# Attention sinks as bf16 products of three parts, split on GpSimd and VectorE, and ranks as sums of signs on ScalarE

## The chip, the core and the metric

The kernel runs on one core of a Trainium2 chip. A core has a matrix engine (TensorE; PE in the profile, with PEld for the loads of its weights), a vector engine (VectorE, DVE), an activation engine (ScalarE, ACT), a general-purpose engine (GpSimd, POOL) and a queue engine (SyncE, SP). Each runs its own instructions in the order in which they were issued; semaphores tie them together. DMA transfers are issued from the queues of SP, ACT and POOL. The metric is the time of one execution on the device, in microseconds; lower is better.

## The reference

Attention with a sliding window and four sinks for 4 batches of 8 heads, 768 positions of 64 values; then a mixture of depths: in each batch the 128 rows with the highest gate score go through a two-layer network, and the others are left as they are.

```python
scores = scale * np.matmul(q, k.transpose(0, 1, 3, 2))
keep = is_sink | in_window            # first 4 positions, or the last 128
scores = np.where(keep, scores, -1000000000.0)
a = np.exp(scores - np.max(scores, axis=-1, keepdims=True))
a = a / (np.sum(a, axis=-1, keepdims=True) + 1e-09)
x = np.matmul(a, v)                   # heads side by side: B, S, 512
...
scores = np.einsum('bsd,d->bs', x, w_gate)
top_idx = np.argpartition(-scores[b], capacity)[:capacity]
h = np.maximum(x[b, top_idx] @ w1, 0.0)
g = 1.0 / (1.0 + np.exp(-scores[b, top_idx]))
out[b, top_idx] = x[b, top_idx] + g[:, None] * (h @ w2)
```

## The kernel before

The work is written out in a fixed order of 30 entries, the list `steps`. Batch 0 takes entries 0 to 11, with two of the four head groups at a time (g = 0, then g = 1, for each of six blocks of 128 queries); batches 1 to 3 take six entries each, all heads at once (12 to 17, 18 to 23, 24 to 29). The loop over `steps` (L728 to L763) does the same in each entry: a store of the rows finished before, the scores of the entry two ahead (`step_scores`, with one or two exponentials of 1024 columns on ACT, L296), then `values` (the products of probabilities and values, fp32, L307, and of the sinks, L318, into PSUM banks X and X+1, the same in every entry), then `norm` (a reciprocal, L347, and two multiplications, L350, on DVE), then the gate score of the finished rows (L354). Other work is hung on an entry by four lists: `before` (ahead of the entry), `middle` (ahead of `values`), `at` (behind `norm`) and `late` (at the end).

**Loads and transposes.** K and Q of a pair of heads come by `load_pair` (L150, on SP's queue) into `raw`, are cast to bf16 on POOL (`cast_pair`, L185), turned by PE (`transposes`, L52) into PSUM banks Y and Y+1, and copied from there to KT and QT by DVE or ACT (L222, L224). The loads are held back by a list `plan`: its k-th group is issued once 188 + 256 k units of PE work have been issued (`Counted`; an fp32 product counts four, a bf16 product or a transpose two), which is called mark k.

**Sinks.** `sink_keys` (L231, POOL) copies the first four columns of KT into `ksk`, so that one product with Q gives the scores of the sinks of several heads, 64 rows for each half of the query columns. `sink_scores` does these products and one exponential into `psk` (fp32). The values of the sinks lie in `vsk` (fp32, rows 0 to 15, loaded by four DMAs of POOL's queue, L521; the copy for rows 64 to 79 is made by POOL, L725). In `values`, `sinks()` multiplies 64 rows of both; in all entries that have sinks, but for one, these are the first products of the entry.

**Ranks.** A row is chosen if fewer than 128 scores of its batch are higher. For batches 0 and 1 the gate scores go to DRAM and come back as a row on all partitions (`bounce_out`, `bounce_in`); `rank_c` (L364, DVE) counts, for each of six columns, how many of 768 are greater. For batches 2 and 3 the row is made by PE (`spread`) and compared block by block (`compare`, `overtake`). `select` and `chosen` make the indices; `gather`, `ffn_*`, `ffn_out` and `scatter` do the network and write the chosen rows over those in DRAM. `gate` and `gate_end` make the sigmoid from the chosen scores, `token_cols` puts a score into two bf16 columns.

**The end.** Behind the loop stands the selection of batch 3, the rest of batch 2's network, `ffn_out(1)` and `scatter(1)`, then those of batches 2 and 3. All scatters write `out` and are done one after the other.

Of the kernel before, what the change touches and what calls it, by code (L numbers as in the profile page):

```python
# [15 lines left out]
B = 4  # L16
H = 8
S = 768
# [37 lines left out]
def kernel(  # L56
# [29 lines left out]
    vsk = one([128, B, 2, HP, SK], FP32, "vsk")  # L86
    ksk = [one([128, HP, 64], BF16, f"ksk{i}") for i in range(2)]
# [5 lines left out]
    pskb = [one([128, 2, 5 * 64], FP32, f"psk{i}") for i in range(2)]  # L93
    x0 = one([128, NB, DM], FP32, "x0")
    scolb = [one([128, NB], FP32, f"scol{i}") for i in range(B)]
    xb = x0[:, 0:NB // 2, :].bitcast(BF16).rearrange("p a (t n) -> p (a t) n", t=2)
    E2 = x0[:, NB - 1, :].bitcast(BF16)[:, 0:NB * 128].rearrange("p (c n) -> p c n", n=128)
    sbc = one([128, S], FP32, "sbc")
    sbl = one([128, S], FP32, "sbl")
# [3 lines left out]
    rankl = [one([128, NB], FP32, "rankl"), x0[:, NB - 2, 40:40 + NB]]  # L103
# [9 lines left out]
    hT = one([128, 8, 128], BF16, "hT")  # L113
    w1_sb = one([128, 4, FF], BF16, "w1_sb")
# [5 lines left out]
    zb = one([128, 512], BF16, "zb")  # L120
# [7 lines left out]
    tk_i = one([128, B + 1, NB], I32, "tk_i")  # L128
    flat = out.rearrange("b s d -> (b s) d")
    srow = tc.dram_tile([B, S], FP32, name="srow")  # L130
    xrow = tc.dram_tile([S, DM], FP32, name="xrow")
    idl = x0[:, NB - 2, 0:1].bitcast(U32)

    class State:
        def __init__(self, b):
            self.b = b
            self.KT, self.QT = KTb[b % 2], QTb[b % 2]
            self.ksk = ksk[b % 2]
            self.v = vbuf[b % 2]
            self.scol = scolb[b]  # L140
            self.psk = pskb if b == 0 else [pskb[(b + 1) % 2]] * 2
# [84 lines left out]
    def sink_keys(b, hp):  # L226
        s = st[b]
        for e in range(2):
            r = slice(64 * e, 64 * e + 64)
            c0 = NSINK * (2 * (hp % 2) + e)  # L230
            pool.tensor_copy(out=s.ksk[r, hp, c0:c0 + NSINK], in_=s.KT[r, hp, 0:NSINK])  # L231

    def sink_scores(b, hps, which, bank):
        s = st[b]
        for hp in hps:
            g = hp // 2
            mine = [h for h in hps if h // 2 == g]
            for c in range(2):
                o = 64 * (g ^ c)
                q2 = s.QT[:, hp, 128:S].rearrange("p (j c n) -> p j c n", c=2, n=64)[:, :, c, :]  # L240
                pe.matmul(out=ps[o:o + 64, bank + c, 0:320], lhsT=s.ksk[:, hp, :], rhs=q2,
# [56 lines left out]
    def values(b, j, heads, bank, which):  # L298
# [13 lines left out]
        def sinks():  # L312
            for be in range(2):
                for c in range(2):
                    if j < 2 - c:
                        continue
                    r = (LO, HI)[be ^ c]
                    pe.matmul(out=ps[64 * c:64 * c + 64, bank + be, a * SK:z * SK],  # L318
                              lhsT=s.psk[which][r, c, 64 * (j - 1):64 * j], rhs=vsk[r, b, be, a:z, :],
# [40 lines left out]
    def bounce_in(b):  # L360
        pool.dma_start(out=sbc[:, :], in_=srow[b, :].partition_broadcast(128))

    def rank_c(b, c):
        dve.tensor_scalar(out=junk[:, :].bitcast(BF16)[:, 0:S], in0=sbc[:, :], scalar1=st[b].scol[:, c:c + 1],  # L364
                          scalar2=0.0, op0=ALU.is_gt, op1=ALU.add, accum_out=rank[:, c:c + 1])
# [39 lines left out]
    def token_cols(b, c0=0, c1=NB):  # L405
        t, sc = tok[b][:, c0:c1, :], st[b].scol[:, c0:c1]
# [430 lines left out]
```

## Time and profile before

| | |
|---|---|
| three runs | 147.26, 144.94, 147.16 us; median 147.16 |
| profiled execution | 144.75 us |
| its span on the engines | 142.8 us, 6432 instructions |
| PE busy | 121.2 us (85%) |
| DVE busy | 92.8 us (65%) |
| ACT busy | 77.6 us (54%) |
| POOL busy | 63.2 us (44%) |
| mean granted PE clock | 0.956 |
| DMA | 32.42 MB, 227 GB/s |

The costliest groups of instructions (line, engine, operation, output and inputs with their shapes, number | busy us, mean ns | idle time before them and what ended most of it):

```profile
L296 ACT ACTIVATE pt<-ps 128x1024 f32<-128x1024 f32 x48 | 47.2, 1025 | 14.7 <-PE ps L49 14.6
...
L49 PE MATMUL ps<-vbuf,pt 64*64 64x65 f32 (+1 forms) x1440 | 47.6, 232 | 0.9 <-issue 0.5
L185 POOL CAST kq<-raw 128x768 bf16<-128x768 f32 x28 | 24.8, 893 | 29.1 <-DMA raw<-in_k_dram 17.7
...
L350 DVE TENSOR_TENSOR x<-ps,rz 128x256 f32<-128x256 f32 (+1 forms) x60 | 19.5, 366 | 1.2
...
L49 PE MATMUL ps<-vsk,psk 64*64 64x260 f32 (+1 forms) x180 | 16.1, 366 | 0.6 <-DVE x L350 0.6
...
L364 DVE TENSOR_SCALAR_CACHE_REDUCE junk<-sbc,scol 128x768 bf16<-128x768 f32 x12 | 12.1, 1012 | 1.3 <-DMA sbc<-srow 0.9
```

All PE products carry the line of the wrapper, L49, and the transposes L52, so they are told apart by their tiles: `vsk,psk` are the products of the sinks, `vbuf,pt` those of the values, `QT,KT` the scores. An fp32 product shows as two instructions. The busy time of PE counts overlapping products once; many run side by side in quarters or halves of the array (the `64*64` in a line).

### The profile page before, as it was taken

How to read it: one execution, taken by the hardware profiler on the slowest of the kernel's cores; microseconds unless marked ns; L12 is line 12 of the kernel's file. 1: busy time of each engine (PE TensorE's matmuls, PEld its weight loads, DVE VectorE, ACT ScalarE, POOL GpSimd, SP SyncE). 2: the span in 40 equal slices, each digit the busy share in tenths (PEclk: the TensorE clock that was granted, in tenths of full speed). 3: DMA queues.
4: the chain of work that ended last, by engine and by line, in shares of the span. 5: the costliest groups of instructions: out<-in, count | busy, mean ns of one | idle time of the engine just before them, and what ended most of it. 6: DMA issues, size and time to landing. Idle time of an engine off the chain costs nothing. (4 is left out here: it accounts for less than half of the span.)

```text
span 142.8 us, 6432 instructions
## 1 busy us (share of the span) xinstructions
PE 121.2 (85%) x2763; PEld 92.6 (65%) x2763; DVE 92.8 (65%) x295; ACT 77.6 (54%) x106; POOL 63.2 (44%) x109
## 2 busy tenths in 40 slices
PE   6768989499998799999699579997999979999900
PEld 2347666478777578777577448776787758676800
DVE  6881643337847474696999623889996888784510
ACT  1577736466978877845857540675744624233100
POOL 7968520698418263141655070634150465225220
PEclk9999999969999999999999955999999999999996
DMA  3998959996999998899686997699998674341311
GB/s 101 358 221 313 276 121 258 392 349 175 318 312 339 264 326 232 211 333 309 239 236 178 287 184 228 144 193 202 260 279 189 230 276 155 145 154 25 122 73 73
DMA packets 42300, 32.42 MB, mean 227 GB/s; under 512 B 26897, under 2 KB 37137, under 8 KB 42273
## 3 DMA queue, kind: packets, MB, share of 16 engines
q1 hardware_dynamic: 38528, 26.22, 62.1%
q0 software_dynamic: 2656, 5.02, 15.5%
q10 hardware_dynamic: 1088, 0.79, 1.8%
q8 instruction: 21, 0.34, 0.9%
q14 instruction: 7, 0.05, 0.1%
HBM read 25.20 MB, written 8.92 MB: 239 GB/s over the span
## 5 line engine op out<-in xcount | busy, mean ns | idle before, releaser
L296 ACT ACTIVATE pt<-ps 128x1024 f32<-128x1024 f32 x48 | 47.2, 1025 | 14.7 <-PE ps L49 14.6
L49 PEld LDWEIGHTS ps<-vbuf,pt 64*64 64x64 f32 (+1 forms) x1440 | 40.9, 140 | 12.0 <-issue 8.8
L49 PE MATMUL ps<-vbuf,pt 64*64 64x65 f32 (+1 forms) x1440 | 47.6, 232 | 0.9 <-issue 0.5
L185 POOL CAST kq<-raw 128x768 bf16<-128x768 f32 x28 | 24.8, 893 | 29.1 <-DMA raw<-in_k_dram 17.7
L347 DVE RECIPROCAL rz<-ps 128x8 f32<-128x8 f32 (+1 forms) x30 | 5.9, 197 | 30.9 <-PE ps L49 30.7
L49 PE MATMUL ps<-QT,KT 64*64 64x192 bf16 (+2 forms) x384 | 18.5, 247 | 3.0 <-ACT sbl L370 0.9
L52 PE MATMUL ps<-ident_b,kq 128*128 128x128 bf16 x192 | 15.4, 228 | 6.0 <-POOL kq L185 3.7
L350 DVE TENSOR_TENSOR x<-ps,rz 128x256 f32<-128x256 f32 (+1 forms) x60 | 19.5, 366 | 1.2
L52 PEld LDWEIGHTS <-kq 128*128 128x128 bf16 x192 | 11.8, 102 | 9.9 <-POOL kq L185 4.4
L354 DVE CUSTOM_DVE_ANT_0 junk<-x,wgb 128x512 f32<-128x512 f32 x24 | 17.7, 736 | 0.5
L49 PE MATMUL ps<-mask,ident_b 64*64 64x256 bf16 (+2 forms) x224 | 16.6, 259 | 0.7 <-issue 0.7
L49 PE MATMUL ps<-vsk,psk 64*64 64x260 f32 (+1 forms) x180 | 16.1, 366 | 0.6 <-DVE x L350 0.6
L49 PEld LDWEIGHTS <-KT 64*64 64x64 bf16 x384 | 11.4, 108 | 6.8 <-issue 4.9
L224 ACT COPY QT<-ps 128x768 bf16<-128x768 bf16 x14 | 11.3, 809 | 4.6 <-PE ps L52 3.7
L364 DVE TENSOR_SCALAR_CACHE_REDUCE junk<-sbc,scol 128x768 bf16<-128x768 f32 x12 | 12.1, 1012 | 1.3 <-DMA sbc<-srow 0.9
L231 POOL COPY ksk<-KT 64x4 bf16<-64x4 bf16 x32 | 6.3, 197 | 13.8 <-DMA xe<-out_dram,idx 5.1
L370 ACT COPY sbl<-ps 128x128 f32<-128x128 f32 x12 | 3.1, 262 | 13.0 <-PE ps L49 12.9
L49 PEld LDWEIGHTS <-ident_b 64*64 64x64 bf16 x240 | 9.4, 111 | 0.9 <-issue 0.9
L222 DVE COPY KT<-ps 128x768 bf16<-128x768 bf16 x8 | 7.6, 953 | 1.7 <-PE ps L52 1.7
L49 PEld LDWEIGHTS ps<-vsk,psk 64*64 64x64 f32 x180 | 6.9, 135 | 2.7 <-DVE x L350 0.9
L49 PE MATMUL ps<-xeT,w_sb 128*128 128x128 bf16 x128 | 7.9, 219 | 0.0
L49 PE MATMUL ps<-w_sb,hT 128*128 128x512 bf16 (+1 forms) x40 | 7.6, 337 | 0.0
(100 smaller groups left out, 135.7 us busy)
## 6 DMA issues: line engine op xcount, KB each, us to landing
out_dram<-x SPq DMA_DIRECT2D x24, 256.0 KB, 4.5
raw<-in_k_dram SPq DMA_DIRECT2D x14, 384.0 KB, 5.4
raw<-in_q_dram SPq DMA_DIRECT2D x14, 384.0 KB, 5.2
vbuf<-in_v_dram SPq DMA_DIRECT2D x33, 128.0 KB, 5.2
w_sb<-in_moe_w_dram POOLq DMA_DIRECT2D x8, 256.0 KB, 7.1
xrow<-x SPq DMA_DIRECT2D x6, 256.0 KB, 3.3
vbuf<-in_v_dram SPq DMA_DIRECT2D x2, 384.0 KB, 5.4
sbc<-srow POOLq DMA_DIRECT2D x2, 384.0 KB, 5.8
```

The lines of the kernel that those rows point to most:

```text
L49: self.counted(self.engine.matmul(**kw), 4 if kw["lhsT"].dtype == FP32 else 2)
L52: self.counted(self.engine.transpose(**kw), 2)
L185: (eng or pool).tensor_copy(out=o, in_=i)
L222: dve.tensor_copy(out=o, in_=i)
L224: act.copy(out=o, in_=i)
L231: pool.tensor_copy(out=s.ksk[r, hp, c0:c0 + NSINK], in_=s.KT[r, hp, 0:NSINK])
L296: act.activation(out=po[:, gi, :, :, :], in_=sc[:, :, :, :], func=ACT.Exp, scale=0.125)
L347: dve.reciprocal(out=rz[:, :, 0:n, :], in_=xg[:, :, :, D:D + 1])
L350: dve.tensor_tensor(out=xo[:, e, :, :], in0=xg[:, e, :, 0:D], in1=rz[:, e, 0:n, :].to_broadcast((128, n, D)), op=ALU.mult)
L354: dve.tensor_tensor_reduce(out=junk[:, :], in0=x, in1=wgb[:, :], scale=1.0, scalar=0.0, op0=ALU.mult, op1=ALU.add, accum_out=st[b].scol[:, ...
L364: dve.tensor_scalar(out=junk[:, :].bitcast(BF16)[:, 0:S], in0=sbc[:, :], scalar1=st[b].scol[:, c:c + 1], scalar2=0.0, op0=ALU.is_gt, op1=A ...
L370: act.copy(out=sbl[:, j * 128:(j + 1) * 128], in_=ps[:, bank, 0:128])
```

## The change

Five things change together.

1. **Sinks of batches 1 to 3.** Values and probabilities of the sinks are each split into bf16 parts whose sum is the fp32 number, and the parts are laid over 128 rows (eight groups of 16), so that one bf16 product over 128 rows takes the place of an fp32 product over 64. `sink_keys` writes eight copies of the columns; `sink_parts` computes one pair of head pairs at a time and its exponential; `sink_split` makes the parts of half of the query columns with four DVE operations (`in_parts`). The values are loaded by a memset and eight DMAs on POOL ahead of entry 2 (`sink_values`), doubled to 32, 64 and 128 rows by two ACT copies (`sink_rows_double`) and split on POOL with four operations a batch, at the end of entries 6, 9 and 14 (`sink_value_parts`). Batch 0 keeps its way; its memset, loads and copy shrink to its own part.
2. **Ranks of batches 0 and 1** are ACT's sum of the sign of the difference, one activation a column, with `rank_end` on DVE; batch 1's row goes to a buffer of its own.
3. **Order.** The transposes of batch 1 move from entries 6, 7, 8, 9 to 8, 8, 9, 9, with their casts; `plan` is rewritten (K and Q earlier, V later for batch 1).
4. **Gate.** The sigmoid is taken in `token_cols` for all rows and its two bf16 parts are chosen along; `gate` is one addition and `gate_end` is gone.
5. **The end.** `ffn_out(1)` and `scatter(1)` move ahead of the last selection.

```diff
-    vsk = one([128, B, 2, HP, SK], FP32, "vsk")
-    ksk = [one([128, HP, 64], BF16, f"ksk{i}") for i in range(2)]
+    vsk0 = one([128, 2, HP, SK], FP32, "vsk0")
+    vskb = [None] + [one([128, 2, HP, SK], BF16, f"vskb{i}") for i in range(1, B)]
+    ksk = [one([128, HP, 128], BF16, f"ksk{i}") for i in range(2)]
+    parts = one([128, 4], FP32, "parts")
...
+        n = 4 if b == 0 else 8
         for e in range(2):
             r = slice(64 * e, 64 * e + 64)
             c0 = NSINK * (2 * (hp % 2) + e)
-            pool.tensor_copy(out=s.ksk[r, hp, c0:c0 + NSINK], in_=s.KT[r, hp, 0:NSINK])
+            o = s.ksk[r, hp, 0:16 * n].rearrange("p (n c) -> p n c", n=n)
+            if b == 0:
+                pool.tensor_copy(out=o[:, 0, c0:c0 + NSINK], in_=s.KT[r, hp, 0:NSINK])
+            else:
+                pool.tensor_copy(out=o[:, :, c0:c0 + NSINK],
+                                 in_=s.KT[r, hp, 0:NSINK].unsqueeze(1).to_broadcast((64, n, NSINK)))
+
+    def in_parts(x, rough, out, row, eng):
+
+        eng.tensor_scalar(out=rough, in0=x, scalar1=parts[:, row:row + 1], scalar2=0.0, op0=ALU.mult, op1=ALU.add)
+        eng.tensor_tensor(out=x, in0=x, in1=rough, op=ALU.add)
+        eng.tensor_scalar(out=rough, in0=x, scalar1=parts[:, row + 1:row + 2], scalar2=0.0, op0=ALU.mult, op1=ALU.add)
+        eng.tensor_tensor(out=out, in0=x, in1=rough, op=ALU.add)
+
+    def sink_parts(b, g, bank):
+        s = st[b]
+        for hp in (2 * g, 2 * g + 1):
+            for c in range(2):
+                q2 = s.QT[:, hp, 128:S].rearrange("p (j c n) -> p j c n", c=2, n=64)[:, :, c, :]
+                pe.matmul(out=ps[:, bank + c, 0:320], lhsT=s.ksk[:, hp, :], rhs=q2, start=hp % 2 == 0,
+                          stop=hp % 2 == 1, skip_group_check=True)
+        x = pskb[0][:, :, :]
+        act.activation(out=x, in_=ps[:, bank:bank + 2, 0:320], func=ACT.Exp, scale=0.125)
+
+    def sink_split(b, g, c):
+        in_parts(pskb[0][:, c, :], xe[2][:, 0:160].bitcast(BF16), st[b].pskh[:, g, c, :], 0, dve)
...
-                    r = (LO, HI)[be ^ c]
-                    pe.matmul(out=ps[64 * c:64 * c + 64, bank + be, a * SK:z * SK],
-                              lhsT=s.psk[which][r, c, 64 * (j - 1):64 * j], rhs=vsk[r, b, be, a:z, :],
+                    if b:
+                        lhsT, rhs = s.pskh[:, be, c, 64 * (j - 1):64 * j], vskb[b][:, be, a:z, :]
+                    else:
+                        r = (LO, HI)[be ^ c]
+                        lhsT, rhs = s.psk[which][r, c, 64 * (j - 1):64 * j], vsk0[r, be, a:z, :]
+                    pe.matmul(out=ps[64 * c:64 * c + 64, bank + be, a * SK:z * SK], lhsT=lhsT, rhs=rhs,
...
-        pool.dma_start(out=sbc[:, :], in_=srow[b, :].partition_broadcast(128))
+        pool.dma_start(out=sbcs[b][:, :], in_=srow[b, :].partition_broadcast(128))
 
     def rank_c(b, c):
-        dve.tensor_scalar(out=junk[:, :].bitcast(BF16)[:, 0:S], in0=sbc[:, :], scalar1=st[b].scol[:, c:c + 1],
-                          scalar2=0.0, op0=ALU.is_gt, op1=ALU.add, accum_out=rank[:, c:c + 1])
+
+        act.activation(out=x0[:, NB - 1, :].bitcast(BF16)[:, 0:S], in_=sbcs[b][:, :], func=ACT.Sign, scale=-1.0,
+                       bias=st[b].scol[:, c:c + 1], accum_out=rank[:, c:c + 1])
+
+    def rank_end():
+        dve.tensor_scalar(out=rank[:, :], in0=rank[:, :], scalar1=-0.5, scalar2=0.5 * (S - 1), op0=ALU.mult, op1=ALU.add)
...
-        t, sc = tok[b][:, c0:c1, :], st[b].scol[:, c0:c1]
-        dve.tensor_copy(out=t[:, :, 2], in_=sc)
-        dve.tensor_tensor(out=t[:, :, 3], in0=sc, in1=t[:, :, 2], op=ALU.subtract)
+
+        t, g = tok[b][:, c0:c1, :], gcol[:, c0:c1]
+        act.activation(out=g, in_=st[b].scol[:, c0:c1], func=ACT.Exp, scale=-1.0)
+        dve.tensor_scalar_add(out=g, in0=g, scalar1=1.0)
+        dve.reciprocal(out=g, in_=g)
+        dve.tensor_copy(out=t[:, :, 2], in_=g)
+        dve.tensor_tensor(out=t[:, :, 3], in0=g, in1=t[:, :, 2], op=ALU.subtract)
...
-        plan = [[lambda: load_pair(0, 3), lambda: load_v_first(2)],
-                [load_gate, P(1, 0), P(1, 1)],
-                [P(1, 2), P(1, 3), V(1, 0)],
-                [P(2, 0), V(1, 1)],
-                [P(2, 1), V(1, 2)],
-                [P(2, 2), V(1, 3)],
-                [P(2, 3), V(1, 4)],
-                [V(1, 5), V(1, 6), V(2, 0)],
-                [P(3, 0), V(2, 1)],
-                [P(3, 1), V(2, 2)],
-                [P(3, 2), V(2, 3)],
-                [P(3, 3), V(2, 4)],
-                [V(2, 5), V(2, 6), V(3, 0), W(0)],
-                [V(3, 1), W(1), W(2)],
-                [V(3, 2), W(3), W(4)],
-                [V(3, 3), W(5), W(6)],
-                [V(3, 4), V(3, 5), W(7)],
-                [V(3, 6)]]
+        plan = [[lambda: load_pair(0, 3), load_gate, lambda: load_v_first(2)],
+                [P(1, 0), P(1, 1)],
+                [P(1, 2), P(1, 3)],
+                [P(2, 0), P(2, 1)],
+                [V(1, 0), V(1, 1), P(2, 2)],
+                [P(2, 3), V(1, 2)],
+                [V(1, 3), V(1, 4), P(3, 0)],
+                [V(1, 5), V(1, 6), P(3, 1)],
+                [V(2, 0), V(2, 1), P(3, 2)],
+                [V(2, 2), P(3, 3)],
+                [V(2, 3), V(2, 4)],
+                [V(2, 5), V(2, 6), W(0)],
+                [V(3, 0), V(3, 1), W(1)],
+                [V(3, 2), W(2), W(3)],
+                [V(3, 3), W(4), W(5)],
+                [V(3, 4), W(6), W(7)],
+                [V(3, 5), V(3, 6)]]
...
-        for b, i, js in ((0, 12, (15, 15, 16, 17, 17, 18)), (1, 18, (20, 21, 22, 23, 24, 25))):
+        for b, i, js in ((0, 12, (15, 16, 16, 17, 17, 18)), (1, 18, (21, 22, 22, 23, 23, 24))):
...
-        for b, i0 in ((1, 6), (2, 12), (3, 18)):
-            for hp in range(HP):
-                before(i0 + hp - 1, lambda b=b, hp=hp: cast_pair(b, hp))
-                middle(i0 + hp, lambda b=b, hp=hp: transposes(b, hp, Y))
-                at(i0 + hp, lambda b=b, hp=hp: sink_keys(b, hp))
-            at(i0 + 4, lambda b=b: sink_scores(b, range(HP), 0, Y))
+        for b, at_ in ((1, (8, 8, 9, 9)), (2, (12, 13, 14, 15)), (3, (18, 19, 20, 21))):
+            for hp, i in enumerate(at_):
+                (late if b == 1 and hp == 3 else before)(i - 1, lambda b=b, hp=hp: cast_pair(b, hp))
+                (at if hp and i == at_[hp - 1] else middle)(i, lambda b=b, hp=hp: transposes(b, hp, Y))
+                at(i, lambda b=b, hp=hp: sink_keys(b, hp))
+            for g in range(2):
+                i = (9, 14, 20)[b - 1] + 2 * g
+                at(i, lambda b=b, g=g: sink_parts(b, g, Y))
+                for c in range(2):
+                    late(i + c, lambda b=b, g=g, c=c: sink_split(b, g, c))
...
+        def sink_values():
+
+            pool.memset(vsf[:, :], 0.0)
+            for r in range(2):
+                for hh in range(HP):
+                    r0 = 16 * r + NSINK * hh
+                    pool.dma_start(out=vs[r0:r0 + NSINK, :, :, hh, 0:D].rearrange("p b e d -> p (b e) d"),
+                                   in_=v4[hh, 0:NSINK, 1:B].rearrange("s b e d -> s (b e) d"))
+
+        def sink_rows_double(n):
+            act.copy(out=vsf[n:2 * n, :], in_=vsf[0:n, :])
...
+        def sink_value_parts(b):
+            n = 2 * HP * SK
+            in_parts(vsf[:, (b - 1) * n:b * n], w2_sb[:, :, :].rearrange("p c f -> p (c f)")[:, 0:n],
+                     vskb[b][:, :, :, :].rearrange("p e h w -> p (e h w)"), 2, pool)
+        before(2, sink_values)
+        for n in (32, 64):
+            late(5, lambda n=n: sink_rows_double(n))
+        late(5, sink_rows)
+        for b, i in ((1, 6), (2, 9), (3, 14)):
+            late(i, lambda b=b: sink_value_parts(b))
...
         compare_own(b, NB - 1)
+        ffn_out(1, Y + 1)
+        scatter(1)
         overtake((NB - 1,), 3)
...
-        ffn_out(1, Y + 1)
-        scatter(1)
         ffn_2(2, 0, 0)
         ffn_2(2, 1, 0)
         ffn_out(2, 0)
         scatter(2)
-        gate_end(b)
         ffn_1(b, 0, Y)
```

Not shown: the setting up of the row masks and of the per-row factors `parts` (`sink_rows`, eleven small POOL operations and two of DVE, at the end of entry 5), buffers that are laid over others, and the two lines that take `gate_end` away.

## The prediction

> **What bounds the kernel now.** I number the 30 entries of `steps` 0 to 29 and mark step i's end by its reciprocal in `norm` (L347), R(i). I read the slices first:
>
> ```profile
> PE   6768989499998799999699579997999979999900
> DVE  6881643337847474696999623889996888784510
> ...
> PEclk9999999969999999999999955999999999999996
> ```
>
> PE is nearly always busy, except around slices 7 and 22, and just behind each hole PEclk falls to half. Windows laid over those places:
>
> ```profile
> 24.80:28.20 3.40, 1.34 (x19) 1.07 (x21) 1.42 (x3) 1.31 (x2) 2.05 (x5) 0.95 1.07 392
> 28.20:31.60 3.40, 3.40 (x46) 2.74 (x43) 1.37 (x5) 1.98 (x3) 3.02 (x5) 0.55 1.05 365
> ...
> 79.20:82.60 3.40, 1.34 (x38) 0.96 (x38) 2.45 (x10) 2.51 (x5) 0.46 (x1) 0.98 1.01 297
> 82.60:86.00 3.40, 2.97 (x35) 2.01 (x37) 0.56 (x4) 1.18 (x2) 2.12 (x4) 0.50 0.93 171
> 86.00:89.40 3.40, 3.40 (x78) 2.94 (x79) 1.33 (x6) 0.27 (x1) 0.00 (x0) 0.51 0.77 230
> ```
>
> (PE, PEld, DVE, ACT, POOL busy; then clock.) About 2 us of idle PE in 3.4 us costs a further 3.4 or 6.8 us at half clock: 1.7 and 3.4 us lost. The waits and the timeline name the cause, input loads that reach POOL's casts late:
>
> ```profile
> POOL kq L185 <- DMA raw<-in_k_dram: 17.7, 8, 4.5
> ...
> PE ps L52 <- POOL kq L185: 3.7, 3, 1.6
> ```
> ```profile
> 20.60 0.40 POOL L231 COPY ksk<-KT 64x4 bf16<-64x4 bf16 x2 [2.21 <-DVE KT L222]
> 22.14 0.46 PE L49 MATMUL ps<-QT,ksk 128*64 128x320 bf16 x4
> 25.48 0.82 POOL L185 CAST kq<-raw 128x768 bf16<-128x768 f32 x1 [4.47 <-DMA raw<-in_k_dram]
> 26.36 0.51 PE L52 MATMUL ps<-ident_b,kq 128*128 128x128 bf16 x6 [1.59 <-POOL kq L185]
> ```
>
> Between the holes PE and DVE alternate, because `values` always writes the same two PSUM banks: it can't start before the previous `norm` is done. Two steps (same columns):
>
> ```profile
> 91.90:95.78 3.88, 3.88 (x107) 2.93 (x108) 3.51 (x11) 2.80 (x4) 2.11 (x5) 1.00 1.07 172
> 95.78:99.49 3.71, 3.00 (x66) 2.26 (x66) 3.57 (x11) 2.18 (x3) 1.43 (x2) 1.00 1.09 178
> ```
>
> DVE fills 3.5 us of 3.7 to 3.9; 1.0 of it is one rank. The end is a row of scatters on POOL, each held until the one before has landed:
>
> ```profile
> 131.13 1.02 POOL L486 DMA_INDIRECT out_dram<-y,idx  x1 [0.30 <-issue]
> ...
> 134.74 1.00 POOL L486 DMA_INDIRECT out_dram<-y,idx  x1 [2.59 <-DVE hT L468]
> ...
> 138.26 0.98 POOL L486 DMA_INDIRECT out_dram<-y,idx  x1 [2.51 <-DMA out_dram<-y,idx]
> ```
>
> **What the Trainium skill says.** "TensorE: Matmul & The Clock Gate", Part 1: after an idle window of about 3.4 us the array runs at half clock. The trace agrees (0.55 and 0.50, in units of 3.4 us). "SBUF — State Buffer", "Who interferes with whom": a VectorE instruction with two SBUF inputs and a GpSimd instruction that reads SBUF exclude one another. The trace fits: the 6-column subtraction of L408 takes 0.77 us beside a cast, where the 5-column one takes 0.17.
>
> **The change, part by part.** The sum is made against the profiled execution: span 142.8, 144.75 us in all, which is 2.4 below the median 147.16 and under all three runs.
>
> *Removed or relieved.*
> - The waits of steps 6 and 7: no transposes stand there any more. Gaps of 1.59 and 0.50, and 1.7 of half clock: **-3.8**.
> - R(20) to R(21) takes 9.32 us (78.68 to 88.00), beside 4.3 for the step before. The last loads of batch 3 are released two marks earlier, so that the cast should find its data: about -4.7.
> - Sinks of batches 1 to 3: 8 instructions of a step take 0.60 us (115.89 to 116.49). In bf16 there are 4, over 128 rows. The fp32 value products have the same two column halves: 64 in 1.64 us, 26 ns each for 65 columns in two passes, so 260 columns in one pass cost twice that, and 4 take 0.2. PE saves 0.4 in each of 13.5 steps. Eight score products per batch go from 64 to 128 columns wide and lose pairing: 0.73 to about 1.1.
> - 12 ranks of 1.03 us leave DVE for ACT. In exchange DVE gets 12 splits of four 128x320 operations. Cast-like: 344 ns at 384, so 0.30; two-input: 419 at 256, so 0.48; a split is 1.55. DVE's work is 4.5, 4.2, 4.3 and 4.4 in steps 20 to 23, where a step took 3.7 to 3.9 apart from the hole; there the PE saving is worth nothing.
> - Step by step, the larger of PE's and DVE's work from R(14) to R(29) is 4.0+3.7+3.5+4.3+3.3+4.4+4.6+4.6+4.6+4.4+4.0+4.9+4.9+3.7+5.0 = 63.9, against 69.0 now (54.57 to 123.60). PE's work is the present step less 0.3 to 0.4, plus 0.5 with `sink_parts`; DVE's is norm 0.98, gate score 0.77, split 1.55, KT copy 0.95, and the comparisons of the trace, where the step has them. **-5.1**, the hole included; R(13) to R(14) **-0.3**.
> - The tail: `scatter(1)` goes out about 4 us earlier, so `scatter(2)` follows its y (132.93) at once, and the last scatter waits for its own y (136.3) instead of 138.26: -1.7. The moved y (0.75, half hidden by a PE wait) and two more gate operations add 0.7 ahead of `chosen`. **-1.0**.
> - Costed at nothing: the smaller start-up memset (DVE waits for POOL's bands until 3.90 in any case); the gate load in front of `load_v_first(2)` (0.54 of SP's queue; those values are needed from step 6, some 5 us after they land; with that cover gone, 0.5); V(1,0) and V(1,1) at mark 4, behind step 9's products: 5.2 to land, about 7 until values(12) asks for them, else the difference is a stall; the weights, a mark earlier on POOL.
>
> *Added.*
> - **A.** POOL gets a memset of 1560 and eight DMAs behind the cast that ends at 18.03, ahead of the `ksk` copies of pairs 1 and 3. Memset: 0.10 for one column, 0.20 for 128, so 1.35. DMAs: L521's median of 0.617, so 4.9. With two times 0.4 for the copies `ksk` is ready at 25.1, and PE, in order, stands at its sink scores from 22.14: **+3.0** (1.1 if issue and memset are a third cheaper), with half clock behind it, **+1.4**.
> - **B.** ACT copies 32 and 64 rows of 1560 once the last DMA has landed (issue at 23.7 + 5.1 = 28.8). 0.81 for 768 and 0.48 for 384 give 1.5 each. The exponential of step 8 queues behind, to 32.7, and values(7) needs it; DVE's column copy waits for the same two, with norm(6) behind it. PE, late by A, would stand there at about 31.5: **+1.1** (0 to 2).
> - **C.** Then POOL splits batch 1's sink values. One-input operations of 520 cost 0.65 by the cast (893 ns at 768); the two-input ones aren't in the trace. "GPSIMD Engine Reference", section 3.1, has 4497 ns at 2048, an estimate of 1.14 at 520 (0.6 if they run like casts). 3.6 in all, with two casts queued behind: step 8's transposes, which PE reaches near 35, wait to about 37.3, and values(8) with them. **+2.2** (0.5 to 4).
> - **D.** Eight PSUM copies of batch 1 lie in steps 8 and 9 instead of four steps. ACT has 1.02 + 3 x 0.8 in each, PE steps are 2.3. Each transpose pair and `sink_parts` wait for the two copies before: 0.6+0.4+1.2, and 0.6 of products: **+2.8**.
> - **E.** The last split of batch 1 stands in late(12), behind norm 0.98, gate columns 1.0 and gate score 0.8; values(13) begins with the sinks. Ready R(12)+4.3; PE has 1.85 of other work. A stall of 2.3 for 0.75 now: **+1.6**; **+0.8** for DVE in steps 10 to 12.
> - One more window at half clock behind C or E: **+1.7** (0 to 5).
> - Twelve signs on ACT: "ScalarE: Activation LUTs", "What ACT_TABLE_LOAD costs", gives 280 + 0.833 N for an activation with a bias column: 0.92. Its other line, 186 + 0.833 N, gives 1.04 for the exponential measured at 1.025, so I believe it. ACT then has 4.5 in steps 15 and 16 and 4.8 in 21 and 22, with exponentials two steps ahead: nothing in the sum (0 to 3).
>
> With X for A to D and the extra window, the sum is X - 3.8 + 2.4 - 5.1 - 0.3 - 1.0 = X - 7.8. X = 3.0+1.4+1.1+2.2+2.8+1.7 = 12.2, so +4.4: 149.2 beside 144.75. Against the median most of the 2.4 comes on top: **151**.
>
> **The rivals.**
> 1. *The early insertions hide* (faster). With A 1.1, B 0, C 0.5, D 1.4 and no half clock, X is 3 and the sum -4.8: 140 beside the profile, **142** by the median. It is over 2% faster from X below 4.9. For it: POOL sits idle for 4.5 us before 25.48, and ACT is lightly used. Against it: `ksk` and the casts stand behind the new work in POOL's one order, so idle time later doesn't help. 0.18.
> 2. *The insertions and the late gain cancel*: X between 4.9 and 10.7, about **147**. That the product doesn't quicken a step at all, because DVE sets it, belongs here: only the hole is gained. 0.17.
> 3. *ACT becomes the bound* in steps 15 to 24 (signs dearer by their accumulator, say 0.2 each, and no slack): +3, **154**. For it: 4.5 and more per step; against: ACT is busy for 2.2 to 2.8 now. 0.13.
> 4. *Cold PE*: A, C and E each bring one or two windows at half clock, +5 beyond the sum, **156**. 0.12.
>
> **How the numbers follow.** My forecast, slower through POOL's and ACT's order in steps 4 to 13, has 0.40; with rivals 3 and 4 that is 0.65 for slower by over 2% (which is about what a measurement of this kernel tells from no change), 0.17 for within, 0.18 for faster. The forecast alone spans 149 to 154; 143.5 to 157.5 takes in half of rival 1 and most of 4.
>
> **What would show it.** A: `ksk` of pairs 1 and 3 after 24, PE waiting for POOL near 22. B: the two ACT copies waiting for a DMA, then PE for ACT. C: PE waiting for casts near 35. D: transposes waiting for QT and KT copies. E: a sink weight load waiting for DVE in step 13. Late: no hole near 80, DVE full in steps 20 to 23. I am wrong if R(10) comes before about 42, or if the ranks' new engine sets the late steps.

## The result and the profile after

The changed kernel takes 164.68 us (median of 4, 163.50 to 164.77) where the kernel before takes 146.14 (median of 4): ratio **1.130** [1.121, 1.140], slower. Its profiled execution took 164.66, span 162.9. The prediction was 151.0, with 143.5 to 157.5 as its range: the direction was right, the size far too small. The kernel before spreads from 141 to 149 us over the executions of this study, so that kernels are best compared within one series, and by stages of the traces. Executions of one kernel fall into a faster and a slower group; ratios use the faster one, and none is given for e5 to e8, in whose series only one of seven executions of the kernel before (141.35 us; median of all 145.43, highest 148.87) belongs to it.

Slices of the page of the kernel after (tenths of busy time, then the granted clock):

```profile
PE   6789838746966784399776888998497998998950
...
DVE  5855420262667999556999877999879559798230
...
PEclk9999995675999789569999999999879999999997
```

Where the kernel before has dips at slices 7 and 22 (counted from 0), there are now dips at slices 5, 8, 12 and 15 to 16; the clock is low behind them. Two of its costliest groups (the columns as before):

```profile
L195 POOL CAST kq<-raw 128x768 bf16<-128x768 f32 x28 | 25.0, 922 | 4.2 <-DMA raw<-in_k_dram 3.4
...
L49 PE MATMUL ps<-vskb,pskA 128*64 128x260 bf16 x36 | 4.8, 291 | 6.4 <-DVE pskA L254 4.7
```

The sink products are cheaper, as meant (those of batches 1 to 3 take 6.9 us, 11.2 before), and POOL is idle for only 4.2 us ahead of its casts, 29.1 before. The waits of the same kernel say what came instead (engine and tile, what released it; us in total, times, longest):

```profile
PE ps L49 <- ACT pt L332: 6.3, 9, 2.1
PE ps L49 <- DVE x L389: 5.6, 6, 2.0
PE ps L49 <- DVE pskA L254: 4.7, 1, 4.7
PE ps L52 <- POOL kq L195: 3.3, 1, 3.3
PE ps L49 <- POOL ksk L244: 2.6, 1, 2.6
```

Gaps of more than 0.15 us in PE's work add up to 31.7 us, 13.9 before, and up to the last products the clock is at half for 27.3 us, 10.2 before. By stages, each from one profiled execution (R(i) as in the prediction; all from R(0) on, since the first loads arrive up to 2.7 us apart):

| us | R(0)-R(8) | R(8)-R(13) | R(13)-R(14) | R(14)-R(29) | rest |
|---|---|---|---|---|---|
| before | 23.0 | 15.6 | 3.6 | 69.0 | 19.2 |
| after | 29.5 | 29.1 | 3.9 | 69.4 | 18.6 |
| after, unaltered once more (e0) | 30.2 | 28.4 | 3.2 | 69.9 | 18.6 |

So the 20 us are lost in steps 0 to 13, and the late stretch, which was to gain 5.1, gains nothing. One execution's stage can be off by some us: in the five traces of kernels whose sinks and transposes are those of the kernel before, R(0) to R(8) lies between 21.7 and 24.8. Of the changed kernel, R(0) to R(13) is 58.6 in both traces.

### The profile page after: what moved, and what is told of

Its sections match the earlier page's. It is cut to its first block, busy times and chain, and to the rows that moved or that the text cites. A ratio compares the mean times of both kernels' runs of the same rounds, so it can differ in the third digit from the quotient of the medians.

```text
span 162.9 us, 6415 instructions
## 1 busy us (share of the span) xinstructions
PE 124.2 (76%) x2709; PEld 96.6 (59%) x2709; DVE 110.8 (68%) x325; ACT 93.0 (57%) x136; POOL 82.5 (51%) x141
## 4 chain that ended last, share of the span: by engine, by line
DVE 22%; PE 21%; DMA 19%; ACT 19%; POOL 8%; issue 7%; POOLq 1%; SPq 0%; ACTq 0%
PE ps L49 17%; ACT pt L332 7%; DMA xe<-out_dram,idx 6%; ACT x L404 6%; DMA raw<-in_q_dram 5%; PE ps L52 4%; DMA out_dram<-y,idx 3%; DVE x L389 3%; DVE junk L393 3%; DMA w_sb<-in_v_dram 3%; DVE psk L252 3%; POOL w_sb L775 2%; DVE xe L251 2%; DVE xe L253 2%; ACT w_sb L779 2%
## 5 line engine op out<-in xcount | busy, mean ns | idle before, releaser
L49 PE MATMUL ps<-vbuf,pt 64*64 64x65 f32 (+1 forms) x1440 | 49.7, 237 | 1.0 <-issue 0.4
L49 PEld LDWEIGHTS ps<-vbuf,pt 64*64 64x64 f32 (+1 forms) x1440 | 44.1, 147 | 6.8 <-issue 3.2
L49 PE MATMUL ps<-QT,KT 64*64 64x192 bf16 (+2 forms) x384 | 19.4, 264 | 3.9 <-ACT pt L332 2.3
L393 DVE CUSTOM_DVE_ANT_0 junk<-x,wgb 128x512 f32<-128x512 f32 x24 | 18.2, 760 | 0.7
L246 POOL COPY ksk<-KT 64x32 bf16<-64x32 bf16 x24 | 6.0, 251 | 18.5 <-DVE KT L232 7.4
L49 PE MATMUL ps<-QT,ksk 128*128 128x320 bf16 (+1 forms) x32 | 6.7, 345 | 5.0 <-POOL ksk L244 2.6
L264 ACT ACTIVATE psk<-ps 128x640 f32<-128x640 f32 x6 | 4.2, 703 | 10.9 <-DVE rz L386 7.4
L49 PE MATMUL ps<-vskb,pskA 128*64 128x260 bf16 x36 | 4.8, 291 | 6.4 <-DVE pskA L254 4.7
L49 PEld LDWEIGHTS <-hT 128*128 128x128 bf16 x53 | 5.2, 104 | 5.6 <-issue 1.8
L842 POOL CAST x<-x 128x512 bf16<-128x512 f32 x6 | 5.3, 879 | 6.0 <-DVE rankl L446 3.4
```

The lines of the kernel that those rows point to most:

```text
L49: self.counted(self.engine.matmul(**kw), 4 if kw["lhsT"].dtype == FP32 else 2)
L246: pool.tensor_copy(out=o[:, :, c0:c0 + NSINK], in_=s.KT[r, hp, 0:NSINK].unsqueeze(1).to_broadcast((64, n, NSINK)))
L393: dve.tensor_tensor_reduce(out=junk[:, :], in0=x, in1=wgb[:, :], scale=1.0, scalar=0.0, op0=ALU.mult, op1=ALU.add, accum_out=st[b].scol[:, ...
L842: pool.tensor_copy(out=xb[:, j, :], in_=x)
```

## The experiments

My theory: the orders on POOL, ACT and DVE around the change of batch (A to E) make the early loss, and the late gain is absent because splits are dearer than I took them and signs stand ahead of exponentials. Rivals: cold PE; DVE's or ACT's sum of work, wherever it stands.

**Undo A to C by order (e1).**
```diff
-        before(2, sink_values)
+        late(3, sink_values)
...
-            late(5, lambda n=n: sink_rows_double(n))
-        late(5, sink_rows)
-        for b, i in ((1, 6), (2, 9), (3, 14)):
+            late(8, lambda n=n: sink_rows_double(n))
+        late(8, sink_rows)
+        for b, i in ((1, 9), (2, 10), (3, 14)):
```


> The changed kernel with the new work of batch 1 moved back in POOL's and ACT's order: memset and eight DMAs behind the ksk copies of step 3, the two ACT copies and the row pattern behind step 8, the sink values of batch 1 split behind step 9. If parts A to C of the prediction (the order on POOL and ACT) make the early loss, PE no longer waits 2.6 us at 22.4 nor 3.3 us at 34.7, R(10) falls from 53.5 to between 44 and 48, and the time from 164.7 to between 156 and 160 us. If that work only displaces the wait (its 4.6 us on POOL then holds the casts of batch 2, or DVE's splits set steps 9 to 13 in any case), R(10) falls but R(14) stays above 72, and the time stays at or above 163 us.

Measured: 161.84 us, ratio 1.126 [1.120, 1.132], between the two; R(10) is 50.3, above the 44 to 48 named, and R(14), at 72.8, fits the second reading. The three waits of A, B and C went: R(0) to R(8) is 20.9. That is 8.5 less than after (what A to C cost, by this pair of traces) and 2.1 less than before; but this execution reached R(0) 2.5 us late, with the later loads that much nearer, so both differences may flatter it. R(8) to R(13) rose to 32.6. In step 9 PE waited 3.4 us for DVE's KT copy, which stood behind a DVE wait of 2.9 us for the row pattern, now on POOL in step 8. And POOL's value splits ran beside two of DVE's splits, which took 3.5 and 4.1 us. R(0) to R(13) falls by 5.0 only.

**Both splits of batch 1's second half in step 11 (e2).**
```diff
-                    late(i + c, lambda b=b, g=g, c=c: sink_split(b, g, c))
+                    late(11 if b == 1 and g else i + c, lambda b=b, g=g, c=c: sink_split(b, g, c))
```


> The changed kernel with both splits of batch 1's second half in the late list of step 11, so that the last one no longer stands behind norm, gate columns and gate score of step 12. If part E (the place of that one split) is what makes PE wait 4.7 us before values(13), the wait falls to 2 us or less and the time from 164.7 to between 160 and 163 us, the half clock behind the wait included. If DVE's sum of work sets steps 10 to 13 wherever the split stands, step 11 to 12 becomes longer by the same 2 to 3 us, and the time stays between 164 and 165.5 us.

162.06 us, 1.127 [1.119, 1.134]. The 4.7 us wait is gone and R(8) to R(13) takes 24.9, though step 11 to 12 grows from 4.0 to 5.9. The time lies in the range of the first reading, but the ratio is hardly below the 1.130 of the changed kernel, and the execution profiled began 2.6 us late: by time alone the gain isn't settled.

**PE kept busy in its waits (e3).**
```diff
+        def warm(i, at_i, n):
+            for m in range(n if i == at_i else 0):
+                o = ps[:, X, 260:512] if at_i == 13 else ps[:, Y, 384:512]
+                nc.tensor.matmul(out=o, lhsT=zb[:, 0:128], rhs=zb[:, 0:252 if at_i == 13 else 128], start=True, stop=True,
+                                 skip_group_check=True)
...
+            warm(i, 8, 50)
...
+            warm(i, 13, 40)
...
+            warm(i, 4, 40)
```


> The changed kernel with dummy products (zero weights, unread PSUM columns) put before PE's waits of step 4 (40 of 128 columns), step 8 (50 of 128) and step 13 (40 of 252), so that PE isn't idle there; nothing else is moved. If the waits are set by POOL's and DVE's queues and the half clock behind them is a second cost, the waits end where they ended before, PE runs at full clock behind them, and the time falls by 3 to 6 us, to between 158.5 and 162. If cold PE is the main cost of the change, the time falls by 8 us or more, below 157. If PE isn't what sets those stretches, the time stays above 163.5.

166.12 us, 1.155 [1.148, 1.162]: no gain, and my own expectation of 3 to 6 us fell too. The clock is at half for 20.5 us instead of 27.3, and R(0) to R(13) is 59.1, after 58.6. Step 5 became shorter by 1.3 us (0.4 beside e0), and the next wait, for DVE behind ACT's copies, took it: 3.8 us, after 1.25 (3.0 in e0). So the half clock that was taken away was not what ended last; the 20.5 us that stayed are not tested by this.

**Ranks back on DVE (e4).**
```diff
-        act.activation(out=x0[:, NB - 1, :].bitcast(BF16)[:, 0:S], in_=sbcs[b][:, :], func=ACT.Sign, scale=-1.0,
-                       bias=st[b].scol[:, c:c + 1], accum_out=rank[:, c:c + 1])
+        dve.tensor_scalar(out=junk[:, :].bitcast(BF16)[:, 0:S], in0=sbcs[b][:, :], scalar1=st[b].scol[:, c:c + 1],
+                          scalar2=0.0, op0=ALU.is_gt, op1=ALU.add, accum_out=rank[:, c:c + 1])
```


> The changed kernel with the twelve ranks of batches 0 and 1 back on DVE as comparisons (1.03 us each), and none on ACT. If DVE with its splits is what sets the late steps and the signs only take slack on ACT, R(14) to R(29) grows from 69.4 to between 73 and 78 and the time from 164.7 to between 168 and 174 us. If ACT is the bound of the late steps (signs ahead of the exponentials in its order), that stretch becomes shorter, 63 to 67, and the time falls to between 159 and 163 us.

172.57 us, 1.201 [1.196, 1.205]; R(14) to R(29) 76.9. With the splits there, DVE has no room for ranks.

**No splits on DVE (e5).**
```diff
-        act.activation(out=x, in_=ps[:, bank:bank + 2, 0:320], func=ACT.Exp, scale=0.125)
+        act.activation(out=s.pskh[:, g, :, :], in_=ps[:, bank:bank + 2, 0:320], func=ACT.Exp, scale=0.125)
...
-        in_parts(pskb[0][:, c, :], xe[2][:, 0:160].bitcast(BF16), st[b].pskh[:, g, c, :], 0, dve)
+        pass
```


> The changed kernel without DVE's splits: the exponential writes the bf16 weights directly, and the twelve groups of four DVE instructions are left out (so the sinks of batches 1 to 3 are not the reference's; every product, transpose, POOL split and sign stays). If DVE's splits, which stand between norms, are what steps 9 to 13 and the late steps pay, PE's waits of 2.0 and 4.7 us there go, R(9) to R(13) falls from 24.8 to between 13 and 17 us, R(14) to R(29) from 69.4 to between 63 and 67, and the ratio to the kernel before from 1.13 to between 1.02 and 1.06. If the packed transposes, ACT's order and the half clock pay, R(9) to R(13) stays above 20 and the ratio above 1.09.

153.95 us beside 145.43 (141.35 to 148.87), so the ratio lies between 1.06 and 1.09 and settles nothing. R(8) to R(13) is 18.4: **the splits and their waits are worth 10.7 us** of that stretch, and what is left over the kernel before is 2.8. In e12 below, the same kernel up to step 13, it is 20.3, with one more stretch at half clock: 8.8 and 4.7. The stretch that I named, R(9) to R(13), is 14.1, as in the first reading. R(14) to R(29) stays at 68.5, outside it: late, the splits aren't the bound alone.

**A to D undone together (e6).**
```diff
-        for b, at_ in ((1, (8, 8, 9, 9)), (2, (12, 13, 14, 15)), (3, (18, 19, 20, 21))):
+        for b, at_ in ((1, (6, 7, 8, 9)), (2, (12, 13, 14, 15)), (3, (18, 19, 20, 21))):
...
-                (late if b == 1 and hp == 3 else before)(i - 1, lambda b=b, hp=hp: cast_pair(b, hp))
+                before(i - 1, lambda b=b, hp=hp: cast_pair(b, hp))
...
-        before(2, sink_values)
+        late(3, sink_values)
...
+            late(8, lambda n=n: sink_rows_double(n))
+        late(8, sink_rows)
+        for b, i in ((1, 9), (2, 11), (3, 14)):
```


> The changed kernel with parts A to D undone together: the transposes of batch 1 back in steps 6, 7, 8 and 9 with their casts before them, memset and DMAs behind the ksk copies of step 3, ACT's copies and the row pattern in step 8, sink values of batch 1 split behind step 9. Left are DVE's splits, their place (E), and the late part. If A to D are worth what the trace of the changed kernel shows of them (6.6 us by step 8 and some 3 in steps 8 and 9), R(0) to R(13) falls from 58.6 to between 46 and 51 us and the ratio from 1.13 to between 1.05 and 1.08. If DVE's splits beside POOL's value splits set steps 9 to 13 wherever the rest stands, R(0) to R(13) stays above 52 and the ratio above 1.09.

162.58 us beside 145.43. R(0) to R(13) is 55.2: the second reading. Again both value splits of POOL ran beside DVE's, which took 3.9 and 4.4 us. But the new places bring waits of their own, so this isn't A to D taken away: in step 6 PE waits 3.4 us for casts that stand on POOL behind the memset and the eight DMAs (22.1 to 28.3), and at 43.7 another 2.0 for ACT's KT copy.

**Signs alone in the kernel before (e7).** `rank_c` by signs with `rank_end`, in the changed kernel's steps.


> The kernel before with one part of the change alone: the ranks of batches 0 and 1 as sums of signs on ACT, in the steps of the changed kernel. If DVE is the bound where it has a rank (3.5 us of work in steps of 3.7 to 3.9) and ACT has slack, R(14) to R(29) falls from 69.0 to between 63 and 67 and the ratio lies between 0.96 and 0.985. If the signs hold up the exponentials behind them (as at 112 to 114 us of the changed kernel), PE waits for ACT instead, and the ratio is 0.99 or more.

145.99 us beside 145.43, R(14) to R(29) 68.7: no gain. PE waits for exponentials behind pairs of signs (1.8 us near 95, 1.7 near 99). R(20) to R(21) is 5.5 us here, with the loads of the kernel before.

**Loads and tail alone (e8).**
```diff
-                [P(2, 3), V(1, 4)],
-                [V(1, 5), V(1, 6), V(2, 0)],
-                [P(3, 0), V(2, 1)],
-                [P(3, 1), V(2, 2)],
-                [P(3, 2), V(2, 3)],
-                [P(3, 3), V(2, 4)],
+                [P(2, 3), V(1, 4), P(3, 0)],
+                [V(1, 5), V(1, 6), P(3, 1), V(2, 0)],
+                [P(3, 2), V(2, 1)],
+                [P(3, 3), V(2, 2)],
+                [V(2, 3)],
+                [V(2, 4)],
```
(and `ffn_out(1)`, `scatter(1)` as in the change)


> The kernel before with two parts of the change that have nothing to do with the sinks: the loads of batch 3's pairs two marks earlier, and batch 1's output and scatter ahead of the last comparison. If the hole at step 21 (R(20) to R(21) of 9.3 us) is held by those loads, it falls to 5.5 us or less, with the half clock behind it; with 1 us of the tail the ratio lies between 0.95 and 0.975. If the hole is held by POOL's order (gather and ksk copies) rather than by the load, it stays near 9 and the ratio lies between 0.985 and 1.0.

142.40 us (141.78 to 147.61) beside 145.43: not told apart. The hole is 5.5 us, but so it is in e7 without the loads, and R(14) to R(29) is 69.0, as before.

**The changed kernel once more, and POOL's split of batch 2 moved away (e0, e11).**


> The changed kernel unaltered, so that the other kernels of this series have it beside them on their chip: a ratio to the kernel before between 1.12 and 1.14, R(9) to R(13) near 24.8 us, R(14) to R(29) near 69.4.


```diff
-        for b, i in ((1, 6), (2, 9), (3, 14)):
+        for b, i in ((1, 6), (2, 13), (3, 14)):
```


> The changed kernel with one move: POOL splits the sink values of batch 2 behind step 13 instead of step 9, so that DVE's first split of batch 1 no longer runs beside it. If the two engines hold each other up in SBUF (the split took 3.8 us beside POOL's operations, 1.85 where POOL was idle), the first split falls to 2.3 us or less, PE's wait of 2.0 us in step 10 to below 0.8, and the unaltered changed kernel loses 1.5 to 4 us. If the split's time is DVE's own, it stays above 3.3 us and the time within 1 us of the unaltered one.

In one series: e0 165.52 us, 1.164 [1.150, 1.178]; e11 162.23, 1.142 [1.131, 1.153]. The ratio of e0 is above the 1.12 to 1.14 that I expected; its time is within 1 us of the first series, so it is mainly the kernel before that was faster here. The first split of the kernel after, beside POOL (timeline: start, us, engine, line, operation):

```profile
49.00 1.17 POOL L252 TENSOR_TENSOR w_sb<-w_sb 128x520 f32<-128x520 f32 x1
...
49.69 0.66 DVE L251 TENSOR_SCALAR xe<-psk,parts 128x320 bf16<-128x320 f32 x1 [2.13 <-ACT psk L264]
...
50.27 0.70 POOL L253 TENSOR_SCALAR w_sb<-w_sb,parts 128x520 bf16<-128x520 f32 x1
50.39 0.92 DVE L252 TENSOR_TENSOR psk<-psk,xe 128x320 f32<-128x320 f32 x1
...
51.05 1.28 POOL L254 TENSOR_TENSOR vskb<-w_sb 128x520 bf16<-128x520 f32 x1
51.34 1.18 DVE L253 TENSOR_SCALAR xe<-psk,parts 128x320 bf16<-128x320 f32 x1
...
52.55 0.99 DVE L254 TENSOR_TENSOR pskA<-psk,xe 128x320 bf16<-128x320 f32 x1
```

and the second of e11, with POOL idle:

```profile
54.11 0.38 DVE L251 TENSOR_SCALAR xe<-psk,parts 128x320 bf16<-128x320 f32 x1
54.53 0.49 DVE L252 TENSOR_TENSOR psk<-psk,xe 128x320 f32<-128x320 f32 x1
55.06 0.39 DVE L253 TENSOR_SCALAR xe<-psk,parts 128x320 bf16<-128x320 f32 x1
55.48 0.49 DVE L254 TENSOR_TENSOR pskA<-psk,xe 128x320 bf16<-128x320 f32 x1
```

3.85 us against 1.86, the same four operations. Each of the first three ends 0.2 to 0.3 us behind the POOL operation that runs beside it. In e11 the first split met POOL's casts instead and took 2.8, not below 2.3; PE's wait of 2.0 us in step 10 fell to 1.0, not below 0.8. The gain of 3.3 us is in the range of the first reading. The value split of batch 2 now ran beside the split of step 12, which took 3.1 us, 2.4 in e0, and PE's wait in step 13 was 5.0: the collision was moved, not removed.

**One sign per step (e9).**
```diff
-        for b, i, js in ((0, 12, (15, 16, 16, 17, 17, 18)), (1, 18, (21, 22, 22, 23, 23, 24))):
+        for b, i, js in ((0, 12, (14, 15, 16, 17, 18, 19)), (1, 18, (20, 21, 22, 23, 24, 25))):
```


> The changed kernel with its twelve signs one per step (14 to 19 and 20 to 25) instead of singly and in pairs. If pairs of signs that stand ahead of the exponentials on ACT are what keeps the late steps from being shorter, PE's waits for ACT of 0.9 and 2.1 us go and R(14) to R(29) falls from 69.4 to between 65 and 68 us; it doesn't fall further because DVE has 4 us and more in steps 15, 16 and 20 to 25. If a sign costs its 1.05 us wherever it stands, or DVE's splits are the bound, R(14) to R(29) stays between 68.5 and 71.

162.06 us, 1.141 [1.130, 1.152], beside e0's 165.52. R(14) to R(29) is 67.0, 2.9 less. What went, in the timeline of the kernel after:

```profile
113.31 0.94 ACT L404 ACTIVATE x<-raw,scol 128x768 bf16<-128x768 f32 x1
114.15 0.19 ACT L404 ACTIVATION_READ_ACCUMULATOR x<-raw,scol 128x1 f32 x1
114.24 1.92 ACT L332 ACTIVATE pt<-ps 128x1024 f32<-128x1024 f32 x2
...
116.21 0.38 PE L49 MATMUL ps<-ident_f,scol 128*128 128x128 f32 x1 [2.06 <-ACT pt L332]
```

It is the second sign of its step: the exponentials start when it is done, and PE 2.1 us late. In e9 PE's waits for ACT's exponentials are 3.9 us in all and 1.0 at the longest, after 6.3 and 2.1.

**An attempt to beat both (e10).** The kernel before with e8's two parts and every second rank as a sign, in the kernel before's steps.


> The kernel before with what was found harmless: batch 3's pair loads two marks earlier, batch 1's output and scatter ahead of the last comparison, and every second rank as a sign on ACT, the others left on DVE, never two signs in one step. If ACT and DVE each have room for half of the ranks, R(14) to R(29) falls from 69.0 to between 62 and 65.5 us and the ratio lies between 0.955 and 0.985. If a sign costs PE as much as a comparison on DVE, the stretch stays above 66 and the ratio between 0.985 and 1.01.

141.87 us, 0.999 [0.990, 1.009]; R(14) to R(29) 68.5. No gain: this is the second reading, in which a sign costs PE about what a comparison did.

**Neither splits nor pairs of signs (e12)**: e5 and e9 in one.


> The changed kernel without DVE's splits (the exponential writes the bf16 weights directly, so the sinks of batches 1 to 3 are not the reference's) and with the signs one per step. If splits on DVE and pairs of signs on ACT are two bounds side by side that hide the late gain, R(14) to R(29) now falls to between 62.5 and 65.5 us, about the 63.9 of the prediction. If TensorE or single signs set the late steps in any case, it stays above 66.

1.088 [1.076, 1.100]; R(14) to R(29) 65.9, just outside both readings and close to the second. With neither splits nor pairs of signs the kernel is still 9% slower than the kernel before. Three waits ahead of value products, for which the profile names no releaser (1.3, 1.0 and 0.7 us), are in it; without them it would be 62.8. That is arithmetic, not a run.

**All causes repaired (e13)**: transposes as in e6, memset and DMAs in `late(3)`, ACT's copies and rows in `late(7)`, value splits behind steps 8, 13 and 14, signs as in e9, and e15's edit.


> The changed kernel, complete, with every named cause repaired at once: memset and DMAs behind the ksk copies, transposes of batch 1 in steps 6 to 9, sink values of batch 1 split behind step 8 and those of batch 2 behind step 13 (away from DVE's splits), the sinks of values(13) multiplied last, the signs one per step. If the causes add up, R(0) to R(13) falls from 58.6 to between 44 and 49 us, R(14) to R(29) to between 66 and 68.5, and the ratio to between 1.03 and 1.07. If a repaired wait only turns up as another one, R(0) to R(13) stays above 52 and the ratio above 1.09.

156.18 us, 1.087 [1.067, 1.107]: outside both readings, at the edge of the second. R(0) to R(13) is 51.8 and R(14) to R(29) 66.0, but R(13) to R(14) grows to 6.0, most of it at half clock. By the ratios (1.130 and, in another series, 1.164 for the changed kernel) between a third and a half of the loss is repaired. What came instead is, in the first place, POOL's order again: in step 6 PE waits for a cast that stands right behind the memset and the eight DMAs. The cast has no idle time before it; in the kernel before it had waited for its load, until 25.5.

```profile
23.23 4.50 POOL L775 DMA_DIRECT2D w_sb<-in_v_dram  x8 [0.30 <-POOL w_sb L771]
...
27.77 1.59 POOL L195 CAST kq<-raw 128x768 bf16<-128x768 f32 x2
...
28.65 0.51 PE L52 MATMUL ps<-ident_b,kq 128*128 128x128 bf16 x6 [3.42 <-POOL kq L195]
```

In step 9 it waits 2.1 us for a cast behind the row pattern, and in step 13 still 3.3 for the last split.

**The kernel before once more (e14).**


> The kernel before, unaltered, profiled a second time. If the 9.3 us from R(20) to R(21) were an arrival of loads in the one execution that was profiled, they are 4 to 6.5 us here and R(14) to R(29) lies between 63 and 66.5. If the hole belongs to the kernel, it is 8 us or more here as well.

1.008 [0.989, 1.026]. R(20) to R(21) is 6.4 us: the 9.3 was that of one execution. But R(14) to R(29) is 72.3 here, far above the 63 to 66.5 of that reading, since other waits came in, ahead of value products (1.2 us near 57, 2.0 near 67). The profile names no releaser for them; that they are late loads of V is likely and not shown.

**The sinks of step 13 last (e15).**
```diff
-        first = b == 0 and j == 1 and which == 0
+        first = j == 1 and which == 0 and b < 2
```


> The changed kernel with one move: in values(13) the sink products, which wait for the last split, are issued behind the 64 value products instead of ahead of them. If the place of that split is what PE pays in step 13, the wait of 4.7 us (3.8 in the second execution) falls below 1.5 us, and R(12) to R(13) from 9.2 to between 5 and 7 us. If norm and gate work on DVE hold up step 13 in any case, R(12) to R(13) stays above 8.

161.87 us, 1.134 [1.118, 1.149]. R(12) to R(13) is 5.5 us, in the range of the first reading. PE in the kernel after, then in e15:

```profile
62.69 0.30 PE L49 MATMUL ps<-vskb,pskA 128*64 128x260 bf16 x1
67.68 0.43 PE L49 MATMUL ps<-vskb,pskA 128*64 128x260 bf16 x1 [4.69 <-DVE pskA L254]
```
```profile
64.17 1.78 PE L49 MATMUL ps<-vbuf,pt 128*64 128x65 f32 x64
...
68.11 0.30 PE L49 MATMUL ps<-vskb,pskA 128*64 128x260 bf16 x1 [1.94 <-DVE pskA L254]
```

The products of the values now stand in the wait; what is left of it, 1.9, is over the 1.5 I had named.

## Why the prediction was wrong

The sum was +4.4 us against the profiled execution; the span grew by 20.1. Term by term, each measured figure from one pair of traces:

| step of the prediction | forecast | measured | by |
|---|---|---|---|
| A with its half clock, B, C | +7.7 | +8.5 | R(0)-R(8), after less e1 |
| waits of steps 6 and 7 gone | -3.8 | -2.1 | e1 less before |
| D, packed transposes | +2.8 | +2.8 (4.7) | R(8)-R(13), e5 (e12) less before |
| E, +0.8, a further window at half clock | +4.1 | +10.7 (8.8) | after less e5 (e12) |
| R(13) to R(14) | -0.3 | +0.3 | after less before |
| late steps, hole included | -5.1 | +0.4 | after less before |
| tail | -1.0 | -0.6 | after less before |

**A to D came as forecast in mechanism, and about in size.** A: `ksk` was ready at 25.0, and PE waited for it 2.6 us from 22.4. B: ACT's copies stood behind the DMA, 1.5 us each, DVE's column copy behind them, and PE behind the norm that followed (3.0 us in e0):

```profile
29.12 3.01 ACT L779 COPY w_sb<-w_sb 32x1560 f32<-32x1560 f32 x2 [1.42 <-DMA w_sb<-in_v_dram]
...
32.17 0.19 DVE L804 COPY w_sb<-own 128x24 f32<-128x24 f32 x1 [2.51 <-ACT w_sb L779]
...
32.81 0.63 PE L49 MATMUL ps<-vsk,psk 64*64 64x130 f32 x4 [1.25 <-DVE x L389]
```

C: the casts stood behind 4.7 us of POOL's split (3.6 forecast), and PE waited 3.3 us near 35. R(10) came at 53.5, not before 42. The size of D is a subtraction only, and that the tabled sizes of A to C agree to 1 us is partly luck, since e1 began late. e6, which was to confirm A to D together, doesn't: it moved their work ahead of other casts.

**E is the step that failed: its cost was forecast at 4.1 us and is 8.8 to 10.7.** Two stalls make it.
- In step 10 PE stood 2.0 us, where the sum had +0.8 for three steps. The split of step 9 was priced at 1.55 us and took 3.85 beside POOL's value split; with that moved away (e11) it took 2.8, and the stall was 1.0.
- "A stall of 2.3" in step 13 was 4.7 (3.8 in e0). The last split was ready 5.8 us after R(12), not 4.3: it took 2.8 us beside POOL's casts instead of 1.55, and the gate columns 1.6 instead of 1.0. And PE had 1.2 us of other work, not 1.85. e2 and e15 show that it is the place of this split that PE pays.

Behind the two stalls the clock was at half for 3.4 and 6.8 us, where one window had been allowed for; how much of that counts is open (e3).

A split takes 1.86 us even with POOL idle, and 2.4 on average over the twelve. The prediction had named the very rule of the Trainium skill, "SBUF — State Buffer", "Who interferes with whom", and seen it in the trace, and then priced the splits as if POOL were idle, though the change sets POOL to split values in step 9. The page also says that the one-input form (`tensor_scalar`) can contend; the 1.18 us of such an operation beside POOL, 0.39 with POOL idle, agrees. e1 and e6 gained little partly for this reason (their first two splits took 7.6 and 8.3 us together, 6.3 in the changed kernel), partly because the moved work held up something else.

**The late gain failed** at two steps. "Nothing in the sum (0 to 3)" for the signs: spreading them gains 2.4 us against the first trace and 2.9 against e0, because pairs stand ahead of exponentials. The 0.92 of the formula was near (0.94), but each sign brings an accumulator read of 0.19, and a second sign starts 1.05 us after the first, as rival 3 had it. And "about -4.7" for the hole was read from one execution. In e14 and e7, which have the loads of the kernel before, R(20) to R(21) is 6.4 and 5.5 us. The late stretch with those loads is nevertheless 69 to 72 us: in e14 steps 15, 17, 26 and 28 take 1.1 to 2.3 us more each. In the changed kernel PE waits for no cast there (1.6 us before), but 5.9 us for exponentials and 1.7 for DVE. Taking the splits away as well (e12 after e9) gains a further 1.1; the last 2.0 us down to the 63.9 of the sum, which took the larger of PE's and DVE's work and no wait, are not explained (e12 has 3.0 us of waits there without a named releaser). How long the stretch is without any wait for loads is seen in no run.

**The rivals.** Cold PE (rival 4) is not shown as a cost of its own: taking 6.8 us of half clock away gained nothing (e3). The prediction's "the trace agrees" on idle windows is loose: in the window 79.20:82.60 PE had 1.34 us of work, and the clock fell to half all the same. ACT as a bound (rival 3) is right for a part, 2.4 to 2.9 us, not for the early loss. Rival 1 was far off.

Between a third and a half of the loss has a repair that was seen to work (e13). The rest, 9% above the kernel before, holds splits that still run beside POOL's work, and the memset and DMAs that still stand ahead of casts. Their shares stay open; and since the kernel without any split of DVE's (e12) is 9% slower too, the splits can't be all of it.

## What to carry to other kernels

Before an operation is priced for DVE, ask what POOL will be doing in the same microseconds after the change: here that doubled a split. Undoing one cause in a pinned order shifts the others against each other, and work that is moved stands ahead of something else; so measure by stages and take parts out altogether before believing a sum of waits. And a hole that is seen in one execution is not yet a property of the kernel: look for it in a second trace before counting its end as a gain.

## What the runs showed of the hardware

- A DVE operation on 128x320 took 0.38 to 0.49 us with POOL idle and up to 1.39 beside POOL's operations on 128x520; POOL's own, 1.17 us for two inputs, rose to 1.28 to 1.52 in the trace of the changed kernel.
- An activation with an accumulator output is two entries, 0.94 and 0.19 us; a second one started 1.05 us after the first, an exponential 0.93 after.
- Keeping PE busy with dummy products cut the half-clock time by 6.8 us (27.3 to 20.5) and the kernel's time by nothing (166.12 us, 1.155).
- Eight small DMAs issued by POOL held its order for 4.50 us (L775), and casts queued behind them.
